# Attention and MoE on one core: moving low-part subtractions from GpSimd to VectorE

## The chip, the core and the metric

The kernel runs on one core of a Trainium2 chip. Its engines have a queue each and run side by side: TensorE (PE in the profile; PEld are its weight loads), VectorE (DVE), ScalarE (ACT), GpSimd (POOL), and SyncE (SP), which issues the DMAs. The metric is the device time of one execution in microseconds (us).

## The reference

A block-sparse attention and a feed-forward layer behind it, cut to what is computed:

```python
scores = 0.125 * q @ k.T              # per batch (4) and head (8), 768 x 768, head size 64
scores = where(mask, scores, -1e9)    # band, first and last blocks, 3 sampled blocks per row
attn = exp(scores - max) / (sum + 1e-9)
x = heads_side_by_side(attn @ v)      # 3072 x 512
h = x @ w_in                          # 512 -> 2048
g = where(h >= 1, h, where(h <= -1, 0, (h + 1) ** 2 / 4))
out = g @ w_out                       # 2048 -> 512
```

## The kernel before

All matmuls that matter run in a shortened fp32 format (F32R). A value is split into a high part, which is the value cast to that format, and a low part, which is the value minus the high part; products of two split values are the sum of three matmuls (or of two, where one side holds both parts in its rows).

**Attention.** 32 heads, one after the other. For each head, matmuls (L267) give all scores into the `pa` buffers, VectorE takes row maxima of them (L272, twelve per head), joins them (L276), TensorE turns them (L280), and VectorE writes them as rows of the operand QA (L283, once per head; the first head has two). Only then can the head's final scores (L303, L304) start; ScalarE takes exponentials (L308) into `pt`. For heads of pairs 0 to 4, the first ten (called whole), these go straight into the product with v in full precision (L333). For the other 22 heads, ScalarE casts the high part ph (a line of the helper `rounded`, L196), VectorE subtracts the low part pl (L316), GpSimd sums the exponentials into `acc` (L323, five per half head), and the products with v take two matmuls (L335, L336). v itself is split for these 22 heads: `split` in `head` lets ScalarE cast the high part into half of `vn` and subtracts the low part into the other half (L243). VectorE also adds the two halves of the product (L345), reduces `acc` (L358), and splits queries and keys (L228) and the results x (L387, L395).

**Weights.** w_in and w_out arrive as 64-bit floats and are converted in 32 pieces of 128x512 (`convert`): a load to `raw`, one step on ScalarE (L168), four on VectorE (L169, L170, L172, L174) in a buffer `cva` of which there are two, then `split`: ScalarE casts the high part into `wi` (w_in, 16 pieces, kept on the chip) or `w` (w_out, 16 pieces, written to DRAM behind it by L448), and the low part is subtracted (L180). The buffer `cva` is free when that subtraction is done; ScalarE's L168 of the piece after next waits for it.

**Feed-forward.** For each half of a batch, 16 steps: matmuls (L457 to L459) into `hp`, ScalarE and VectorE form g (L463, L466, L469), cast it (L196) and subtract its low part gl (L478), and L485 to L487 multiply with `w`. The first half of the first batch runs while w_out is still being converted.

**What sets the order.** `at` puts every step on a plan with a due time, and the steps are issued by due time. A scheduler then puts each engine's instructions into one fixed queue, by these priorities and its own picture of when operands and buffers are ready. On an engine, an instruction that waits holds up everything behind it. So a change of engine alone also changes the order.

Of the kernel before, what the change touches and what calls it, by code (L numbers as in the profile page):

```python
# [13 lines left out]
ALU = mybir.AluOpType  # L14
# [23 lines left out]
def body(ctx, tc, qk_t, v, sampled_blocks, moe_w_in, moe_w_out, ind, cm, negd, ident, fold, out):  # L38
    nc = tc.nc
# [11 lines left out]
    op = pool("op", 1)  # L51
# [21 lines left out]
    def f(ap):  # L73
        return ap.bitcast(F32)
# [82 lines left out]
    def convert(t, src, dst, done=None):  # L157
        st = {}

        def load():  # L160
            st["raw"] = cv.tile([128, 512, 2], I32, name="raw", bufs=3)
            Q_RAW.dma_start(out=st["raw"], in_=src.bitcast(I32).rearrange("p (c w) -> p c w", w=2))

        def bits():
            raw = st["raw"]
            lo32, hi32 = raw[:, :, 0], raw[:, :, 1]
            a = st["a"] = cv.tile([128, 512], I32, name="cva", bufs=2)
            nc.scalar.activation(out=f(a), in_=f(hi32), func=AF.Abs)  # L168
            nc.vector.tensor_scalar(out=f(a), in0=f(a), scalar1=CLO, scalar2=CHI, op0=ALU.max, op1=ALU.min)  # L169
            nc.vector.tensor_scalar(out=a, in0=a, scalar1=3, scalar2=0x3FFFFFFF,  # L170
                                    op0=ALU.logical_shift_left, op1=ALU.bitwise_and)
            nc.vector.scalar_tensor_tensor(out=a, in0=hi32, scalar=-0x40000000, in1=a,  # L172
                                           op0=ALU.bitwise_and, op1=ALU.bitwise_or)
            nc.vector.scalar_tensor_tensor(out=a, in0=lo32, scalar=29, in1=a,  # L174
                                           op0=ALU.logical_shift_right, op1=ALU.bitwise_or)

        def split():
            hi, lo = dst()
            rounded(CH, hi, f(st["a"]))
            nc.gpsimd.tensor_tensor(out=lo, in0=f(st["a"]), in1=f(hi), op=ALU.subtract)  # L180
            if done:
                done()

        conv.append((t, load, bits, split))
# [5 lines left out]
    def rounded(eng, dst, src):  # L190
        if eng is nc.vector:
            eng.tensor_copy(out=dst, in_=src)
        elif eng is nc.gpsimd:
            eng.tensor_scalar(out=dst, in0=src, scalar1=1.0, scalar2=0.0, op0=ALU.mult, op1=ALU.add)
        else:
            eng.copy(out=dst, in_=src)  # L196

    def head(i, n0, b, h, pst):
# [7 lines left out]
        st = {}  # L206
# [33 lines left out]
        def split(pl, n, src, hi, lo):  # L240
            t = st[n] = pl.tile([128, T, 128], F32R, name="vn")
            rounded(nc.scalar, t[:, :, hi], st[src])
            nc.gpsimd.tensor_tensor(out=t[:, :, lo], in0=st[src], in1=f(t[:, :, hi]), op=ALU.subtract)  # L243

        def v_whole():
            st["vn"] = VW[e]
# [5 lines left out]
        if whole:  # L252
            at(n0 - G["vw"], v_whole)
        else:
            at(n0 - G["vs"], split, vp, "vn", "lv", o0, o1)
# [372 lines left out]
```

## Time and profile before

| | us |
|---|---|
| median of 3 runs | 993.7 (993.34 to 997.28) |
| the profiled execution | 991.61 |
| its span, first to last instruction | 989.8 |
| TensorE busy | 947.2 (96%) |
| VectorE busy | 735.9 (74%) |
| ScalarE busy | 637.2 (64%) |
| GpSimd busy | 323.5 (33%) |

Busy time is the time in which an engine has an instruction under way; instructions that overlap count once. A group of instructions is given with its count, its busy time in sum, the mean of one in ns, and the idle time of its engine just before, with what ended it. Where a stretch of the span is named, it is in us from the first instruction.

### The profile page before, as it was taken

The page shows a single profiled execution, that of the slowest core. Times are in us where ns is not written, and L with a number is a line of the kernel's source. Part 1 is how long each engine was busy: PE and PEld are TensorE (multiplying, and loading weights), DVE is VectorE, ACT ScalarE, POOL GpSimd, SP SyncE. Part 2 cuts the span into 40 slices and gives each one's busy share as a digit, 9 for nine tenths or more (in the row PEclk, how much of TensorE's full clock was granted, in tenths as well). Part 3 has the DMA queues.
Part 4 walks back from the last instruction along what each step waited for, and adds up shares of the span by engine and source line. Part 5 has one row for each costly group of instructions (what it writes and reads, how often), then busy time and mean ns, then how long its engine had stood idle before and what let it go on. Part 6 is the DMA issues. An engine that isn't in the chain of part 4 may idle for free.

```text
span 989.8 us, 14583 instructions
## 1 busy us (share of the span) xinstructions
PE 947.2 (96%) x4687; PEld 830.4 (84%) x4687; DVE 735.9 (74%) x1349; ACT 637.2 (64%) x1302; POOL 323.5 (33%) x283
## 2 busy tenths in 40 slices
PE   5898899999899999999999999999999999999998
PEld 3666567778779989999989999998999899899996
DVE  5888887679998887888888897888888885422222
ACT  3676666666667666777767676866777676533433
POOL 1222120225554344444544444344544444000000
PEclk9999999999999999999999999999999999999999
DMA  6666676753455454656455454655546442434442
GB/s 196 200 182 184 190 207 204 228 180 103 155 170 172 128 141 129 186 151 174 136 143 175 133 150 137 184 158 152 156 130 187 116 124 86 154 128 128 160 128 96
DMA packets 56216, 154.43 MB, mean 156 GB/s; under 512 B 9612, under 2 KB 17952, under 8 KB 56140
## 3 DMA queue, kind: packets, MB, share of 16 engines
q1 hardware_dynamic: 56100, 153.48, 52.1%
q8 instruction: 37, 0.61, 0.3%
q14 instruction: 39, 0.32, 0.1%
q10 hardware_dynamic: 40, 0.03, 0.0%
HBM read 100.92 MB, written 14.81 MB: 117 GB/s over the span
## 4 chain that ended last, share of the span: by engine, by line
PE 70%; DVE 7%; ACT 2%; issue 1%; POOL 0%; POOLq 0%; ACTq 0%; DVEq 0%
PE oa L485 8%; PE oa L487 8%; PE oa L486 8%; PE hp L457 7%; PE hp L458 7%; PE hp L459 7%; PE po L335 5%; PE pa L303 4%; PE pa L304 4%; PE po L336 4%; PE pa L267 4%; DVE pl L316 2%; DVE mc L272 1%; PE pa L459 1%; PE pa L458 1%
## 5 line engine op out<-in xcount | busy, mean ns | idle before, releaser
L323 POOL TENSOR_TENSOR acc<-acc,pt 128x384 f32<-128x384 f32 x176 | 206.6, 1174 | 189.9 <-ACT pt L308 146.2
L272 DVE TENSOR_REDUCE mc<-pa 128x1 f32<-128x384 f32 x384 | 203.3, 549 | 20.4 <-PE pa L267 17.1
L196 ACT CAST ph<-pt 128x384 fp32r<-128x384 f32 x264 | 135.8, 514 | 94.4 <-PE po L335 90.1
L316 DVE TENSOR_TENSOR pl<-pt,ph 128x384 fp32r<-128x384 f32 x264 | 166.9, 632 | 33.3 <-ACT ph L196 32.4
L308 ACT ACTIVATE pt<-pa 128x384 f32<-128x384 f32 x288 | 140.5, 489 | 49.6 <-PE pa L304 41.6
L457 PE MATMUL hp<-x,wi 128*128 128x384 f32 x448 | 156.3, 349 | 5.4 <-DVE r L469 5.3
L485 PE MATMUL oa<-w,gh 128*128 128x512 f32 x384 | 153.3, 399 | 0.3 <-ACT gh L196 0.3
L459 PE MATMUL hp<-x,wi 128*128 128x384 f32 x448 | 152.1, 340 | 0.0
L458 PE MATMUL hp<-x,wi 128*128 128x384 f32 x448 | 152.0, 339 | 0.0
L487 PE MATMUL oa<-w,gl 128*128 128x512 f32 x384 | 151.5, 394 | 0.0
L486 PE MATMUL oa<-w,gh 128*128 128x512 f32 x384 | 150.8, 393 | 0.0
L267 PE MATMUL pa<-KA,QA 88*128 88x384 f32 x384 | 139.4, 382 | 8.8 <-DMA QA<-qkh 5.9
L469 DVE SCALAR_TENSOR_TENSOR r<-r,hp 128x384 f32<-128x384 f32 x112 | 61.8, 552 | 74.6 <-ACT r L466 74.4
L478 DVE TENSOR_TENSOR gl<-r,gh 128x384 fp32r<-128x384 f32 x128 | 91.0, 711 | 30.2 <-ACT gh L196 28.1
L267 PEld LDWEIGHTS pa<-KA,QA 88*128 88x128 f32 x384 | 73.4, 193 | 33.2 <-DVE mc L272 11.2
L303 PE MATMUL pa<-QA,KA 102*128 102x384 f32 x288 | 99.7, 346 | 0.7 <-DVE mc L272 0.4
L463 ACT ACTIVATE r<-hp,half_c 128x384 f32<-128x384 f32 x112 | 65.1, 581 | 52.3 <-PE hp L459 49.2
L304 PE MATMUL pa<-QB,KB 128*128 128x384 f32 x288 | 98.3, 341 | 0.0
L335 PE MATMUL po<-ph,vn 128*128 128x384 f32 x264 | 91.9, 348 | 4.7 <-DVE xun L345 3.9
L457 PEld LDWEIGHTS hp<-x,wi 128*128 128x128 f32 x448 | 85.0, 190 | 12.3 <-DVE r L469 7.8
L323 POOL TENSOR_TENSOR acc<-pt 128x384 f32<-128x384 f32 x44 | 45.6, 1037 | 136.7 <-ACT pt L308 132.9
L336 PE MATMUL po<-pl,vn 128*128 128x384 f32 x264 | 88.8, 336 | 0.0
(97 smaller groups left out, 1665.7 us busy)
## 6 DMA issues: line engine op xcount, KB each, us to landing
w<-wo_dram SPq DMA_DIRECT2D x112, 512.0 KB
qk<-in_qk_t_dram SPq DMA_DIRECT2D x32, 384.0 KB
raw<-in_moe_w_in_dram SPq DMA_DIRECT2D x16, 512.0 KB
raw<-in_moe_w_out_dram SPq DMA_DIRECT2D x16, 512.0 KB
wo_dram<-w SPq DMA_DIRECT2D x16, 512.0 KB
lv<-in_v_dram SPq DMA_DIRECT2D x32, 192.0 KB
KA<-qkh SPq DMA_DIRECT2D x32, 192.0 KB
QA<-qkh SPq DMA_DIRECT2D x32, 192.0 KB
```

The lines of the kernel that those rows point to most:

```text
L267: nc.tensor.matmul(out=pm[:, 0:HALF], lhsT=QAi[0:KM, t * 128:(t + 1) * 128], rhs=KAi[0:KM, kh * HALF:(kh + 1) * HALF], start=True, stop=True)
L272: nc.vector.reduce_max(out=st["mc"][:, t, kh:kh + 1], in_=st.pop(("pm", t, kh))[:, 0:HALF], axis=AX.X)
L308: nc.scalar.activation(out=p, in_=st.pop(("ps", c))[:, 0:HALF], func=AF.Exp, scale=SCALE)
L316: (nc.gpsimd if i < 2 * H and c in PL1 else nc.vector).tensor_tensor(out=pl, in0=st["p", c], in1=f(st["ph", c]), op=ALU.subtract)
L323: nc.gpsimd.tensor_tensor(out=st["acc", hf], in0=prev, in1=st["p", c], op=ALU.add)
L335: nc.tensor.matmul(out=po, lhsT=st["vn"][:, c], rhs=st["ph", c], start=(c == 0), stop=False)
L457: nc.tensor.matmul(out=hv, lhsT=wi[:, j, 0, fs], rhs=x[:, 0], start=(j == 0), stop=False)
L458: nc.tensor.matmul(out=hv, lhsT=wi[:, j, 0, fs], rhs=x[:, 1], start=False, stop=False)
L459: nc.tensor.matmul(out=hv, lhsT=wi[:, j, 1, fs], rhs=x[:, 0], start=False, stop=(j == NP - 1))
L485: nc.tensor.matmul(out=o, lhsT=gh[:, ts], rhs=w[:, 0], start=(fi == 0), stop=False)
L486: nc.tensor.matmul(out=o, lhsT=gh[:, ts], rhs=w[:, 1], start=False, stop=False)
L487: nc.tensor.matmul(out=o, lhsT=gl[:, ts], rhs=w[:, 0], start=False, stop=(fi == NF - 1))
```

## The change

The two subtractions of `split` go to VectorE's queue; what they read and write stays the same. GpSimd keeps the sums L323, and some setting of constants at the start.

```diff
@@ -177,7 +177,7 @@
         def split():
             hi, lo = dst()
             rounded(CH, hi, f(st["a"]))
-            nc.gpsimd.tensor_tensor(out=lo, in0=f(st["a"]), in1=f(hi), op=ALU.subtract)
+            nc.vector.tensor_tensor(out=lo, in0=f(st["a"]), in1=f(hi), op=ALU.subtract)
             if done:
                 done()
 
@@ -240,7 +240,7 @@
         def split(pl, n, src, hi, lo):
             t = st[n] = pl.tile([128, T, 128], F32R, name="vn")
             rounded(nc.scalar, t[:, :, hi], st[src])
-            nc.gpsimd.tensor_tensor(out=t[:, :, lo], in0=st[src], in1=f(t[:, :, hi]), op=ALU.subtract)
+            nc.vector.tensor_tensor(out=t[:, :, lo], in0=st[src], in1=f(t[:, :, hi]), op=ALU.subtract)
```

In the rows of the queues, the number behind QA is its buffer's, mc and mr are a head's maxima, rc holds reciprocals, xun a result before its division, and r the value from which g is formed.

First place: VectorE between a head's last maximum and its L283, the one at 121.45 us in the trace of before. Before:

```order
L272 TENSOR_REDUCE mc<-pa 128x1 x12
L372 RECIPROCAL rc<-rc 24x32
L276 TENSOR_TENSOR mr<-mc 128x6
L172 SCALAR_TENSOR_TENSOR cva<-raw,cva 128x512
L283 TENSOR_TENSOR QA_113<-pa,nd 6x768
```

The same place after:

```order
L272 TENSOR_REDUCE mc<-pa 128x1 x12
L180 TENSOR_TENSOR wi<-cva,wi 128x512
L276 TENSOR_TENSOR mr<-mc 128x6
L174 SCALAR_TENSOR_TENSOR cva<-raw,cva 128x512
L169 TENSOR_SCALAR cva<-cva 128x512
L283 TENSOR_TENSOR QA_113<-pa,nd 6x768
L372 RECIPROCAL rc<-rc 24x32
L180 TENSOR_TENSOR wi<-cva,wi 128x512
```

One subtraction now stands ahead of L276, two steps of a conversion instead of one ahead of L283, and a second subtraction behind it.

Second place: VectorE ahead of the L283 that stands at 278.8 us in the trace of before, while w_out is being converted. Before:

```order
L276 TENSOR_TENSOR mr<-mc 128x6
L369 TENSOR_SCALAR rc<-pa 24x32
L316 TENSOR_TENSOR pl<-pt,ph 128x384
L372 RECIPROCAL rc<-rc 24x32
L283 TENSOR_TENSOR QA_113<-pa,nd 6x768
L316 TENSOR_TENSOR pl<-pt,ph 128x384
L169 TENSOR_SCALAR cva<-cva 128x512
L228 TENSOR_TENSOR qk<-qk,qkh 128x768
```

After:

```order
L276 TENSOR_TENSOR mr<-mc 128x6
L369 TENSOR_SCALAR rc<-pa 24x32
L316 TENSOR_TENSOR pl<-pt,ph 128x384
L372 RECIPROCAL rc<-rc 24x32
L180 TENSOR_TENSOR w<-cva,w 128x512
L316 TENSOR_TENSOR pl<-pt,ph 128x384
L283 TENSOR_TENSOR QA_113<-pa,nd 6x768
L469 SCALAR_TENSOR_TENSOR r<-r,hp 128x384
```

A subtraction and one pl more stand ahead of L283, and r is formed earlier, ahead of the next conversion.

Third place: VectorE in a steady head, behind the end of a half head's product. Before:

```order
L316 TENSOR_TENSOR pl<-pt,ph 128x384
L345 TENSOR_TENSOR xun<-po,otmp 64x384
L478 TENSOR_TENSOR gl<-r,gh 128x384
L316 TENSOR_TENSOR pl<-pt,ph 128x384
L272 TENSOR_REDUCE mc<-pa 128x1 x2
```

After:

```order
L316 TENSOR_TENSOR pl<-pt,ph 128x384
L345 TENSOR_TENSOR xun<-po,otmp 64x384
L243 TENSOR_TENSOR vn<-lv,vn 128x6x64
L478 TENSOR_TENSOR gl<-r,gh 128x384
L316 TENSOR_TENSOR pl<-pt,ph 128x384
L272 TENSOR_REDUCE mc<-pa 128x1 x2
```

The subtraction for v stands alone between L345 and L478; the rest keeps its order. TensorE's order differs in the first quarter of its queue only.

## Rows read from the trace of the kernel before

**Rows 1.** The page's first part: busy time, share, instructions of each engine.
```profile
PE 947.2 (96%) x4687; PEld 830.4 (84%) x4687; DVE 735.9 (74%) x1349; ACT 637.2 (64%) x1302; POOL 323.5 (33%) x283
```

**Rows 2.** By stretch: length, busy PE, PEld, DVE, ACT, POOL; PEclk, DMA, GB/s.
```profile
15.50:153.60 138.10, 124.42 (x490) 88.83 (x490) 119.21 (x226) 92.81 (x187) 26.22 (x19) 0.99 0.68 197
153.60:208.40 54.80, 53.72 (x245) 42.72 (x244) 37.23 (x70) 33.70 (x66) 7.42 (x6) 1.00 0.63 196
208.40:243.40 35.00, 32.28 (x151) 27.92 (x150) 29.22 (x51) 24.04 (x49) 15.87 (x13) 0.95 0.48 149
243.40:278.80 35.40, 31.33 (x145) 25.64 (x144) 35.21 (x55) 21.81 (x46) 18.70 (x15) 0.95 0.48 155
278.80:309.30 30.50, 28.97 (x154) 26.59 (x153) 28.74 (x51) 22.05 (x47) 15.35 (x13) 1.00 0.52 166
309.30:850.00 540.70, 537.39 (x2827) 495.10 (x2826) 441.07 (x811) 382.65 (x797) 236.46 (x210) 1.00 0.50 146
```

**Rows 3.** The chain of waits in 243.4 to 278.8, by engine and line.
```profile
by line: DVE pl L316 18.9%; DVE mc L272 14.5%; issue 12.2%; DVE cva L172 10.3%; DVE cva L174 10.1%; DVE cva L169 6.9%; DVE r L469 5.4%; DVE gl L478 4.4%; DVE cva L170 4.1%; DVE QA L283 2.7%; PE hp L457 1.7%; PE po L335 1.6%; DVE psum L358 1
```

**Rows 4.** GpSimd's groups, whole span: busy us, mean ns, idle before, releaser.
```profile
L243 POOL TENSOR_TENSOR vn<-lv,vn 128x384 fp32r<-128x384 f32 x22 | 24.0, 1089 | 16.6 <-ACT vn L196 16.6
L180 POOL TENSOR_TENSOR wi<-cva,wi 128x512 fp32r<-128x512 f32 x16 | 22.3, 1401 | 96.2 <-ACT wi L196 96.2
```

**Rows 5.** Instructions of a line: duration in ns, least/median/greatest; first and last start.
```profile
L316 DVE TENSOR_TENSOR pl<-pt,ph x264: 482/552/1376, 214.5 to 842.9; 128x384 fp32r<-128x384 f32 x132
L169 DVE TENSOR_SCALAR cva<-cva x32: 399/421/1519, 20.5 to 280.3; 128x512 f32<-128x512 f32 x32
L172 DVE SCALAR_TENSOR_TENSOR cva<-raw,cva x32: 662/692/1651, 24.0 to 283.1; 128x512 int32<-128x512 int32 x32
L174 DVE SCALAR_TENSOR_TENSOR cva<-raw,cva x32: 616/688/1771, 24.9 to 284.2; 128x512 int32<-128x512 int32 x32
```

**Rows 6.** VectorE's groups in 15.5 to 153.6.
```profile
L172 DVE SCALAR_TENSOR_TENSOR cva<-raw,cva 128x512 int32<-128x512 int32 x20 | 15.6, 782 | 0.4
L174 DVE SCALAR_TENSOR_TENSOR cva<-raw,cva 128x512 int32<-128x512 int32 x20 | 15.6, 781 | 0.3
```

**Rows 7.** Instructions in time at 121 to 123: start, duration, idle before.
```profile
121.45 0.95 DVE L283 TENSOR_TENSOR QA<-pa,nd 6x768 fp32r<-6x768 f32 x1
...
122.45 0.45 PE L303 MATMUL oa<-QA,KA 102*128 102x384 f32 x1 [1.35 <-DVE QA L283]
```

**Rows 8.** Waits in 15.5 to 153.6: us in sum, times, longest.
```profile
DVE cva L169 <- ACT cva L168: 8.1, 4, 2.5
...
ACT cva L168 <- POOL wi L180: 6.0, 8, 1.4
```

**Rows 9.** The same in 153.6 to 208.4.
```profile
DVE cva L169 <- ACT cva L168: 10.1, 5, 3.1
```

**Rows 10.** Groups of VectorE, then of GpSimd, in 208.4 to 278.8.
```profile
L316 DVE TENSOR_TENSOR pl<-pt,ph 128x384 fp32r<-128x384 f32 x22 | 17.6, 800 | 1.6 <-ACT ph L196 1.6
...
L172 DVE SCALAR_TENSOR_TENSOR cva<-raw,cva 128x512 int32<-128x512 int32 x6 | 6.3, 1052 | 0.1
L478 DVE TENSOR_TENSOR gl<-r,gh 128x384 fp32r<-128x384 f32 x8 | 6.0, 748 | 1.7 <-ACT gh L196 1.7
L174 DVE SCALAR_TENSOR_TENSOR cva<-raw,cva 128x512 int32<-128x512 int32 x6 | 5.9, 979 | 0.1
...
L169 DVE TENSOR_SCALAR cva<-cva 128x512 f32<-128x512 f32 x6 | 4.0, 659 | 3.4 <-ACT cva L168 3.4
...
L180 POOL TENSOR_TENSOR w<-cva,w 128x512 fp32r<-128x512 f32 x7 | 10.7, 1533 | 11.5 <-ACT w L196 11.5
...
L243 POOL TENSOR_TENSOR vn<-lv,vn 128x384 fp32r<-128x384 f32 x2 | 2.8, 1388 | 0.0
```

**Rows 11.** VectorE's L478 in 309.3 to 850, then in 850 to 989.8.
```profile
L478 DVE TENSOR_TENSOR gl<-r,gh 128x384 fp32r<-128x384 f32 x78 | 60.6, 777 | 8.1 <-ACT gh L196 6.3
...
L478 DVE TENSOR_TENSOR gl<-r,gh 128x384 fp32r<-128x384 f32 x32 | 17.9, 559 | 18.5 <-ACT gh L196 18.4
```

## The prediction

> **What bounds the kernel now.** I read the page's engine shares first: TensorE 96%, VectorE 74%, GpSimd 33% [rows 1]. That is an average over stages with different limits, so the next view is the table of stretches, cut where a head's row of maxima is made (L283) [rows 2]. From 309.3 us to the end TensorE hardly waits: it is busy 537.39 of 540.7 us, while VectorE has 99.6 us idle. So time can only be won or lost ahead of 309.3 us, and there the stretches differ. Stretch one, 15.5 to 153.6: TensorE 124.42 of 138.1, VectorE 119.21; each waits for the other in turn. Stretch two, 153.6 to 208.4: TensorE 53.72 of 54.8, VectorE with 17.6 us idle. Stretch three, 208.4 to 278.8: in its second half VectorE is busy 35.21 of 35.4 us, and TensorE's weight loads fall to 25.64 of 35.4, against 495.10 of 540.7 later [rows 2]. The chain of waits there runs through VectorE: pl 18.9%, mc 14.5%, the conversions' L172, L174 and L169 10.3, 10.1 and 6.9% [rows 3]. So VectorE, which gets the new work, is the bound for some 35 us, half a bound for 170 us, and free otherwise.
>
> The Trainium skill (Trainium Kernel Development and Optimization, Performance Expectations) says that matmul busy time misleads, since matmuls are pipelined, and that the busy share of weight loads tells more. The trace agrees here: in 243.4 to 278.8 the matmuls leave 4.1 us open, the weight loads at the later rate (495.10 of 540.7 is 0.916; 25.64 / 0.916 = 28.0) leave 7.4; by the first a faster VectorE could give back at most 4.1 us there, by the second 7.4.
>
> **What moves, and its price.** 54 subtractions leave GpSimd: 32 of 128x512 (L180; the 16 for wi took 22.3 us) and 22 of 128x384 (L243, 24.0 us) [rows 4]. No row shows L180's form on VectorE. Bounds from the nearest: the 128x384 subtraction L316 has a median of 552 ns, the 128x512 two-input L174 688 ns and L172 692 ns [rows 5]. I take 0.69 for L180, which has L174's size, and 0.55 for L243, which has L316's. All 54 together are 32 x 0.69 + 22 x 0.55 = 34 us of VectorE's time. Three things stand against them: conversions come later in VectorE's queue, VectorE's own instructions are no longer stretched by these GpSimd subtractions, and much lies in idle time.
>
> **Stretch one.** In the new order 16 L180 stand ahead of the head that ends this stretch, but only 17 conversions instead of 20 (counted at L174). Added 16 x 0.69 = 11.0; three conversions less at 2 x 0.421 + 0.692 + 0.688 = 2.22 each (L170, of L169's form, taken at L169's median) [rows 5] take 6.7 away. Relief: L172 and L174 average 782 and 781 ns here, with L180 as GpSimd's main work; 20 x (0.090 + 0.093) = 3.7 [rows 6]. VectorE's load changes by +0.6. On the serial path of a head (last L272, L276, TensorE's turn, L283, first scores) the profile shows that such steps count: L283 takes 0.95 us and TensorE stands 1.35 us for it [rows 7]. With these durations the instructions between the last L272 and L283 grow by 2.8 us over the eight heads (1.5 of it in the last, where there were none; in the diff's first place 0.77), part of it under the turn. Against this, ScalarE waited 6.0 us here for GpSimd to give the cva buffer free, and VectorE 8.1 us for ScalarE's step behind that [rows 8]; a subtraction of 0.69 instead of about 1.29 frees it sooner, where VectorE comes to it at once. I take 0, between -6.0 (all of ScalarE's wait) and +4.3 (11.0 - 6.7, no relief).
>
> **Stretch two.** 8 L180, 1 L243 and three conversions more: 5.5 + 0.55 + 6.7 = 12.8 us. VectorE's 17.6 us of idle time are the cover. But 10.1 of these are waits for ScalarE's L168 [rows 9]; if they stay, 7.5 cover 12.8, and 5.3 show. Below, TensorE's 53.72 of 54.8 allows -1.1. I take 0, as TensorE is the nearer bound.
>
> **Stretch three.** 7 L180 and 2 L243: 4.8 + 1.1 = 5.9, and VectorE is full. Relief: over their medians, L316 stands 22 x 0.248 = 5.5 too long, L172 6 x 0.360 = 2.2, L174 6 x 0.291 = 1.7, L478 8 x 0.189 = 1.5, L169 6 x 0.238 = 1.4, together 12.3 us. Of GpSimd's 15.87 + 18.70 = 34.6 us [rows 2] the subtractions are 10.7 + 2.8 = 13.5, or 39%, and the sums stay; so 4.8 us go [rows 10]. The other 7.5, over these 48 instructions, are 0.16 each; the nine new ones meet the sums alike: 1.4. Net 5.9 - 4.8 + 1.4 = +2.5, and I put all of it on the path. Bounds: +7.3 (no relief), and -3.3 (the first half's 5.8 us of idle time [rows 2] hides that much of the new work, while all relief counts).
>
> **After that.** One L180 and one L243 up to 309.3: 1.2 us, VectorE idle 1.8: 0 to +1.2, taken as 0. The other 18 L243 (9.9 us) go into 99.6 us of idle time; in a steady head each stands between L345 and the gl and pl subtractions, which lose 0.55 but were stretched when GpSimd ran beside them: L478 averages 777 ns there and 559 when GpSimd is silent at the end [rows 11]. TensorE's order is the same there as before. 0. On GpSimd only sums are left, with more room; they are off the path.
>
> Sum: 0 + 0 + 2.5 + 0 = +2.5. The profiled execution took 991.6 us (span 989.8 and 1.8 around it), so 994.1 by its own time. The median of the runs is 993.7, 2.1 above that execution, so 996.2.
>
> **Rivals.** *Slower, VectorE stands still for ScalarE.* The added wait: each L180 needs ScalarE's cast, which is queued behind exponentials. GpSimd waited 96.2 us for it [rows 4] and it cost nothing, as nobody stood behind. Behind VectorE's L180 stand the reductions that free TensorE's score buffers, and L276 and L283. It decides from the point where VectorE reaches L180 before the cast's end. Price: VectorE's nearest wait for ScalarE's part of a conversion is 8.1 us over 20 in stretch one [rows 6, 8], 0.4 each: 16 x 0.4 = 6.4, and 9 x 0.2 = 1.8 in stretch three (0.2 as half of that, an estimate): 996.2 + 8.2 = 1004.4. For it: VectorE is near its limit there. Against: the scheduler put several instructions between cast and subtraction in most places.
>
> *Faster, relief beats load.* All of ScalarE's 6.0 us go, stretch two gives 1.1, stretch three 3.3: 993.7 - 10.4 = 983.3. For it: L172 and L174 stand at 1052 and 979 ns in stretch three [rows 10], and L168 waits for GpSimd. It decides where ScalarE's and VectorE's waits in [rows 8] lie on TensorE's path. Against: the sums stay, and VectorE's load does not fall.
>
> The Trainium skill (SBUF — State Buffer, Who interferes with whom) has a VectorE instruction with two SBUF inputs contend with a GpSimd instruction that reads SBUF, and the loser wait for the whole of the other; the trace agrees, by L478's 777 against 559. By that rule all lengthening in stretch one, where no sums run, goes with the subtractions, which is this rival's condition.
>
> *Slower in the steady heads:* L243 ahead of gl and pl is not hidden: 18 x 0.55 = 9.9, so 1006.1. Against it: VectorE's idle time, and the unchanged order of TensorE.
>
> That the change doesn't do what it says is out: in the built order GpSimd holds nothing but sums behind its start, and VectorE has the 32 and 22.
>
> **How the numbers follow.** A measurement of this kernel tells about 0.5% from no change, 5 us. My forecast of 996.2 is inside that: 0.45. Relief 0.17, and faster by over 0.5%. VectorE standing still 0.33 and the steady heads 0.05, both slower: 0.38. The bounds add up to 983.3 (-10.4) and 1011.8 (4.3 + 5.3 + 7.3 + 1.2 = +18.1); they do not all fall together, and the range of 986 to 1009 holds the rivals' middle and leaves out about 2 in 10.
>
> **What would show it.** Right: VectorE's busy time up by 10 to 20 us from 735.9; L172 and L174 near 0.69 in stretch one; L180 at 0.69 and L243 at 0.55 on VectorE; the head that ended at 153.6 within 4 us of it, the one at 278.8 some 2 to 4 us late; the same pace after 309.3. Wrong: waits of L180 for the casts (wi, w) over 5 us in sum; the head of 153.6 early by more than 4; or TensorE gaps behind 309.3 that grow with each head.

## The result, and the profile after

The changed kernel takes 984.22 us (median of 6 runs, 982.76 to 985.37); the kernel before, run beside it, 993.03 (6 runs, 989.69 to 997.28). The ratio is 0.991, 95% interval 0.9889 to 0.9931: faster by 0.9%, where 996.2 was forecast and 986 to 1009 given as the range. The time lies outside the range, on the other side of no change. The profiled execution took 983.67 us with a span of 981.8, 8.0 less than before.

The page's first part of the kernel after, beside [rows 1]:

```profile
PE 942.5 (96%) x4687; PEld 828.1 (84%) x4687; DVE 747.5 (76%) x1403; ACT 636.5 (65%) x1302; POOL 251.8 (26%) x229
```

and its VectorE groups for the moved work (busy us, mean ns of one, idle time just before, and what ended it), beside [rows 4]:

```profile
L243 DVE TENSOR_TENSOR vn<-lv,vn 128x384 fp32r<-128x384 f32 x22 | 14.1, 640 | 0.4 <-ACT vn L196 0.2
L180 DVE TENSOR_TENSOR w<-cva,w 128x512 fp32r<-128x512 f32 x16 | 10.8, 674 | 0.7 <-ACT w L196 0.7
L180 DVE TENSOR_TENSOR wi<-cva,wi 128x512 fp32r<-128x512 f32 x16 | 10.7, 677 | 4.5 <-ACT wi L196 4.5
```

VectorE is busy 11.6 us longer and the kernel is faster. The prices of the moved instructions are as forecast (0.68 us for L180; L243 has a median of 0.554 us, and a mean of 0.64). The next view is the table by stretch of the kernel after, cut where [rows 2] are cut:

```profile
15.50:153.60 138.10, 128.63 (x519) 94.67 (x519) 121.88 (x239) 94.95 (x192) 0.00 (x0) 0.99 0.65 190
153.60:208.40 54.80, 54.23 (x250) 44.12 (x249) 47.39 (x94) 36.39 (x71) 0.00 (x0) 1.00 0.73 234
...
309.30:850.00 540.70, 537.23 (x2826) 494.63 (x2825) 442.33 (x827) 380.49 (x795) 211.29 (x189) 1.00 0.49 146
```

In the first stretch TensorE gets through 519 matmuls instead of 490, in the second through 250 instead of 245, and behind 309.3 us through as many as before (2826 and 2827). So the gain is made early. The clearest measure of where is equal work: up to which time TensorE has done the first 500, 745, 951, 1050 and 1200 matmuls. Counted by line, these are the same matmuls in both kernels, but for one at 500 and one at 1050. The kernel before, then after (the count stands behind the busy time of PE, and a difference of one is a cut between two starts):

```profile
0.00:154.10 154.10, 128.97 (x500) 91.23 (x501) 127.20 (x247) 97.32 (x193) 29.72 (x28) 0.99 0.68 195
0.00:209.10 209.10, 182.89 (x745) 134.25 (x746) 164.62 (x317) 130.82 (x259) 37.14 (x34) 0.99 0.67 195
0.00:260.40 260.40, 228.11 (x951) 173.53 (x952) 210.11 (x389) 164.83 (x329) 61.09 (x54) 0.98 0.63 187
0.00:282.10 282.10, 249.10 (x1050) 190.24 (x1051) 231.65 (x426) 178.73 (x359) 73.69 (x63) 0.98 0.62 183
0.00:312.40 312.40, 277.88 (x1200) 216.54 (x1201) 260.19 (x475) 201.21 (x406) 89.13 (x75) 0.98 0.61 182
```

```profile
0.00:148.00 148.00, 127.00 (x501) 92.13 (x502) 123.92 (x249) 93.96 (x187) 3.51 (x9) 0.99 0.66 190
0.00:201.70 201.70, 180.13 (x745) 135.29 (x746) 171.86 (x343) 130.79 (x259) 3.51 (x9) 0.99 0.67 201
0.00:249.50 249.50, 223.08 (x951) 171.34 (x952) 215.45 (x415) 164.82 (x329) 19.23 (x22) 0.99 0.64 193
0.00:272.30 272.30, 243.85 (x1050) 188.29 (x1051) 236.88 (x455) 179.28 (x358) 26.15 (x29) 0.99 0.62 186
0.00:304.50 304.50, 273.11 (x1200) 214.34 (x1201) 268.06 (x511) 201.00 (x405) 38.99 (x39) 0.99 0.62 187
```

The differences are -6.1, -7.4, -10.9, -9.8 and -7.9 us. So stretch one gives 6.1, stretch two 1.3, stretch three first 3.5 more and then takes 3.0 back, and nothing happens behind it. TensorE's clock has a part in the 3.5 (see the account of stretch three), but does not make the gain: a second trace of the changed kernel, with the mean granted clock of the kernel before (0.995), has a span of 982.5 us, 7.3 less than 989.8.

What became of the waits of [rows 8] and [rows 9] is in the waits of 15.5 to 153.6 after (us in sum, times, longest):

```profile
DVE wi L180 <- ACT wi L196: 4.5, 4, 1.7
DVE cva L169 <- ACT cva L168: 3.3, 4, 1.9
ACT cva L168 <- DVE wi L180: 1.9, 2, 1.1
```

VectorE stood 8.1 us at L169 for ScalarE's L168, and now 3.3; ScalarE stood 6.0 us for GpSimd there, and now 1.9 for VectorE. In 153.6 to 208.4 VectorE's 10.1 us at L169 [rows 9] are gone altogether. The new wait, L180 for ScalarE's cast, is 4.5 us.

One place shows how that can reach TensorE. The kernel before at 125.5 to 130 (start, duration, engine, line, idle time before and releaser):

```profile
125.55 0.69 DVE L174 SCALAR_TENSOR_TENSOR cva<-raw,cva 128x512 int32<-128x512 int32 x1
125.65 1.73 POOL L180 TENSOR_TENSOR wi<-cva,wi 128x512 fp32r<-128x512 f32 x1 [7.78 <-ACT wi L196]
...
127.41 0.67 ACT L168 ACTIVATE cva<-raw 128x512 f32<-128x512 f32 x1 [1.35 <-POOL wi L180]
...
128.12 0.43 DVE L169 TENSOR_SCALAR cva<-cva 128x512 f32<-128x512 f32 x1 [1.88 <-ACT cva L168]
...
128.92 0.55 DVE L272 TENSOR_REDUCE mc<-pa 128x1 f32<-128x384 f32 x1
...
129.53 0.44 PE L267 MATMUL pa<-KA,QA 88*128 88x384 f32 x1 [0.82 <-DVE mc L272]
```

GpSimd's subtraction takes 1.73 us, during which ScalarE waits for `cva`, VectorE waits for ScalarE, and the first row maxima L272 of the next head stand behind VectorE's L169, although their matmuls (L267) ended in time. This head's L283 came 11.9 us behind its first L267; in the kernel after the same head takes 9.3. Over the eight heads of the stretch the sum of this time fell from 71.8 to 69.5 us, so this one head is all of it; the other half of the 4.4 us that stretch one gained by marks lies between an L283 and the next head's L267.

The 1.73 us are themselves the work of two engines. The least of GpSimd's L180 in this stretch takes 1.27 us; this one began 0.10 us after VectorE's L174, which took its usual 0.69. At 75 us it is the other way round: VectorE's L172 begins 0.16 us after GpSimd's subtraction, takes 1.65 us and ends 0.54 us after it.

```profile
75.14 1.27 POOL L180 TENSOR_TENSOR wi<-cva,wi 128x512 fp32r<-128x512 f32 x1 [1.69 <-ACT wi L196]
75.30 1.65 DVE L172 SCALAR_TENSOR_TENSOR cva<-raw,cva 128x512 int32<-128x512 int32 x1
```

So whichever began first kept its time here, and the other was held up by about as long as was left of it. The means of 782 and 781 ns [rows 6] are not 20 slow instructions each: two of each line took some 1.65 us, the other 18 about 0.69.

The second such place is in SyncE's queue. The kernel before at 87 to 95 (SPq is SyncE issuing DMAs):

```profile
87.41 0.33 SPq L162 DMA_DIRECT2D raw<-in_moe_w_in_dram  x1
87.83 0.47 SPq L221 DMA_DIRECT2D KA<-qkh  x1
88.34 0.59 SPq L221 DMA_DIRECT2D QA<-qkh  x1
...
94.77 0.76 PE L267 MATMUL pa<-KA,QA 88*128 88x384 f32 x3 [1.16 <-DMA QA<-qkh]
```

and the wait ahead of that load in 80 to 95:

```profile
SPq L162 <- DVE cva L174: 5.2, 1, 5.2
```

A late conversion frees `raw` late; the load of 512 KB that waits for it goes out right ahead of the moves of KA and QA, and TensorE has them 6.4 us after QA's issue; it stood 1.16 us for them. In the kernel after no load stands there, and it is 4.4 us:

```profile
88.39 0.59 SPq L221 DMA_DIRECT2D QA<-qkh  x1
...
92.83 0.68 PE L267 MATMUL pa<-KA,QA 88*128 88x384 f32 x3
```

### The profile page after: what moved, and what is told of

Read it like the earlier page. It is cut to its first block, busy times and chain, and to the rows that moved or that the text cites. A ratio compares the mean times of both kernels' runs of the same rounds, so it can differ in the third digit from the quotient of the medians.

```text
span 981.8 us, 14556 instructions
## 1 busy us (share of the span) xinstructions
PE 942.5 (96%) x4687; PEld 828.1 (84%) x4687; DVE 747.5 (76%) x1403; ACT 636.5 (65%) x1302; POOL 251.8 (26%) x229
## 4 chain that ended last, share of the span: by engine, by line
PE 85%; DVE 7%; ACT 3%; DMA 2%; issue 2%; SPq 0%; ACTq 0%; DVEq 0%
PE oa L485 8%; PE oa L487 8%; PE oa L486 8%; PE hp L457 8%; PE hp L459 7%; PE hp L458 7%; PE pa L267 7%; PE pa L303 5%; PE pa L304 5%; PE po L335 5%; PE po L336 4%; PE po L333 4%; DVE mc L272 2%; PE oa L333 2%; DMA QA<-qkh 1%
## 5 line engine op out<-in xcount | busy, mean ns | idle before, releaser
L323 POOL TENSOR_TENSOR acc<-acc,pt 128x384 f32<-128x384 f32 x176 | 201.7, 1146 | 233.0 <-ACT pt L308 195.1
L272 DVE TENSOR_REDUCE mc<-pa 128x1 f32<-128x384 f32 x384 | 202.5, 547 | 19.3 <-PE pa L267 16.1
L316 DVE TENSOR_TENSOR pl<-pt,ph 128x384 fp32r<-128x384 f32 x264 | 163.6, 620 | 34.7 <-ACT ph L196 34.0
L267 PE MATMUL pa<-KA,QA 88*128 88x384 f32 x384 | 138.3, 380 | 5.4 <-DMA QA<-qkh 3.8
L323 POOL TENSOR_TENSOR acc<-pt 128x384 f32<-128x384 f32 x44 | 46.5, 1058 | 345.5 <-ACT pt L308 345.5
L478 DVE TENSOR_TENSOR gl<-r,gh 128x384 fp32r<-128x384 f32 x128 | 84.3, 658 | 24.0 <-ACT gh L196 23.5
L267 PEld LDWEIGHTS pa<-KA,QA 88*128 88x128 f32 x384 | 73.1, 192 | 28.7 <-DVE mc L272 4.7
L335 PE MATMUL po<-ph,vn 128*128 128x384 f32 x264 | 91.4, 346 | 5.1 <-DVE xun L345 3.4
```

The source lines that it names most:

```text
L267: nc.tensor.matmul(out=pm[:, 0:HALF], lhsT=QAi[0:KM, t * 128:(t + 1) * 128], rhs=KAi[0:KM, kh * HALF:(kh + 1) * HALF], start=True, stop=True)
L272: nc.vector.reduce_max(out=st["mc"][:, t, kh:kh + 1], in_=st.pop(("pm", t, kh))[:, 0:HALF], axis=AX.X)
L316: (nc.gpsimd if i < 2 * H and c in PL1 else nc.vector).tensor_tensor(out=pl, in0=st["p", c], in1=f(st["ph", c]), op=ALU.subtract)
L323: nc.gpsimd.tensor_tensor(out=st["acc", hf], in0=prev, in1=st["p", c], op=ALU.add)
```

## The experiments

Three theories stood at first. A: the buffer `cva` comes free sooner. B: VectorE is relieved of GpSimd's subtractions beside it. C: the order alone, in which 17 conversions instead of 20 stand ahead of the tenth L283. Later came D: the loads of raw weights on SyncE's queue. V, in some of the later expectations, is the theory that the number of conversions which VectorE has in stretch one counts; and in the expectation of the second trace the letter C stands for something else, that the change takes away long waits that go with TensorE's half clock. All results in one table; stretch one is the time from the first to the tenth L283 in the profiled execution, the next column from the tenth to the sixteenth, and the fifth column VectorE's wait at L169 for ScalarE's L168 within stretch one. The last two columns are at equal work: the time between the starts of TensorE's 60th and 500th matmul, and of its 500th and 1200th. In brackets stands what TensorE lost in that time at its lower granted clock (1.2 instead of 2.4 GHz), which is half the time at that level. Each of these times is from one execution; the two traces of the changed kernel differ by 1.0, 1.9, 0.3 and 1.9 us in the four columns of times, so a difference of 1 us in stretch one by marks tells nothing.

| kernel | median us | ratio to before (95%) | conversions ahead of the tenth L283 | wait at L169 | stretch one | tenth to sixteenth | matmul 60 to 500 | matmul 500 to 1200 |
|---|---|---|---|---|---|---|---|---|
| before | 991.3 to 993.0 | 1 | 20 | 8.1 | 138.1 | 182.7 | 124.6 (1.7) | 158.4 (3.4) |
| after | 984.22 | 0.991 (0.9889 to 0.9931) | 17 | 3.3 | 133.7 | 179.1 | 118.1 (1.7) | 156.7 (0) |
| after, second trace | 980.81 | 0.9897 (0.9875 to 0.9919) | 17 | 3.1 | 132.7 | 181.0 | 117.8 (1.7) | 158.6 (3.4) |
| weights only | 981.66 | 0.9906 (0.9878 to 0.9933) | 17 | 3.1 | 132.5 | 179.2 | 117.4 (1.7) | 156.8 (1.7) |
| values only | 991.3 | 1.0002 (0.9983 to 1.0022) | 20 | 8.7 | 138.1 | 182.2 | 125.2 (3.4) | 158.0 (1.7) |
| each L180 twice | 986.09 | 0.9937 (0.9914 to 0.996) | 15 | 0 | 131.9 | 182.5 | 117.7 (1.7) | 159.4 (1.7) |
| before, three cva | 988.21 | 0.9967 (0.9946 to 0.9987) | 20 | 1.1 | 136.8 | 183.2 | 122.3 (3.4) | 160.3 (5.1) |
| GpSimd beside | 990.91 | 0.9992 (0.9974 to 1.001) | 17 | 0.6 | 135.1 | 185.3 | 120.6 (1.7) | 162.9 (5.1) |
| GpSimd beside, holding cva | 996.42 | 1.0047 (1.0031 to 1.0063) | 17 | 0.7 | 137.6 | 189.9 | 123.0 (1.7) | 167.5 (8.5) |
| held by a write | 981.33 | 0.9892 (0.9866 to 0.9918) | 16 | 2.8 | 133.3 | 182.4 | 118.1 (3.4) | 159.2 (3.4) |
| GpSimd takes 504 of 512 columns | 987.54 | 0.9953 (0.9937 to 0.9969) | 17 | 2.1 | 133.4 | 184.9 | 119.5 (1.7) | 161.6 (5.1) |
| before, raw loaded once | 973.35 | 0.9814 (0.9786 to 0.9843) | 17 | 0 | 120.3 | 182.5 | 106.9 (0) | 157.3 (5.1) |
| after, six more loads | 987.09 | 0.9955 (0.994 to 0.997) | 18 | 5.2 | 137.1 | 182.3 | 121.1 (1.7) | 160.2 (3.4) |
| weights only, three cva | 978.2 | 0.9866 (0.9845 to 0.9888) | 20 | 0 | 132.9 | 176.7 | 117.2 (1.7) | 154.3 (0) |

**Which half.** The kernel before with only L180 moved, and with only L243 moved.

```diff
-            nc.gpsimd.tensor_tensor(out=lo, in0=f(st["a"]), in1=f(hi), op=ALU.subtract)
+            nc.vector.tensor_tensor(out=lo, in0=f(st["a"]), in1=f(hi), op=ALU.subtract)
```

> Only L180 (weights, 32 subtractions) on VectorE, L243 (values) stays on GpSimd. Three theories share the gain of 8 to 9 us, which the profile shows ahead of 209 us: (A) the conversion buffer comes free sooner, so ScalarE and VectorE wait less; (B) VectorE is no longer lengthened by GpSimd's subtractions; (C) the order alone, with three conversions moved out of the first heads. All three say 984 to 987 here, since L180 is what runs ahead of 209 us and the order of the conversions is that of the changed kernel. If the values carry the gain, 990 to 994.

```diff
-            nc.gpsimd.tensor_tensor(out=t[:, :, lo], in0=st[src], in1=f(t[:, :, hi]), op=ALU.subtract)
+            nc.vector.tensor_tensor(out=t[:, :, lo], in0=st[src], in1=f(t[:, :, hi]), op=ALU.subtract)
```

> Only L243 (values, 22 subtractions) on VectorE, L180 stays on GpSimd. A, B and C: no gain, 991 to 994, the head marks at 153.6 and 208.4 us as before. A gain of over 4 us would speak against all three.

All of the gain is with the weights (0.9906), none with the values (1.0002). The median of the first, 981.66, lies below the 984 to 987 that all three theories gave, and so does the changed kernel's own second median, 980.81.

**What VectorE's load costs.** The changed kernel with each L180 done twice on VectorE: 32 more instructions. In its profile L180 has a mean of 680 ns for wi and 768 for w, so that they are some 23 us.

```diff
             nc.vector.tensor_tensor(out=lo, in0=f(st["a"]), in1=f(hi), op=ALU.subtract)
+            nc.vector.tensor_tensor(out=lo, in0=f(st["a"]), in1=f(hi), op=ALU.subtract)
```

> The changed kernel with each weight subtraction on VectorE done twice: 32 x 0.68 = 22 us more of VectorE's time, no contention, no GpSimd. It prices VectorE's load alone. VectorE has 16.2 us idle in 15.5 to 153.6, 7.4 in 153.6 to 208.4 and is nearly full up to 279: if idle time covers what it can, only the 7 in the last of these show, +5: 989. If it covers nothing, +22: 1006.

The ratio is 0.9937, against 0.991 and 0.9897 in the two comparisons of the changed kernel: 23 us of load cost 2.7 to 4.0 us, where 5 was the least forecast (986.09 against 989), and the intervals of the ratios overlap. Stretch one became no longer (117.7 against 118.1 at equal work), though VectorE's busy time in it rose from 117.62 to 121.82 us (its order has 14 L180 more and two conversions fewer there). Some 4 us more of VectorE's load did not lengthen stretch one.

**The buffer and the contention.** The kernel before with three `cva` buffers; and three forms of the changed kernel in which GpSimd does something in addition behind each cast or subtraction: a subtraction hi - hi into scratch (it reads beside VectorE), the same with `cva` as an operand (it also holds the buffer), and a memset of `cva` (it holds the buffer and only writes).

```diff
-            a = st["a"] = cv.tile([128, 512], I32, name="cva", bufs=2)
+            a = st["a"] = cv.tile([128, 512], I32, name="cva", bufs=3)
```

> The kernel before with three conversion buffers instead of two; the subtractions stay on GpSimd. A: ScalarE's waits of 15 us for GpSimd's release go, and 3 to 5 us of time with them, 986 to 988 where before is 991. If the release matters only where VectorE is loaded too, 990 to 992.

```diff
+            s = cv.tile([128, 512], F32, name="dmy", bufs=2)
+            nc.gpsimd.tensor_tensor(out=s, in0=f(hi), in1=f(hi), op=ALU.subtract)
```

> The changed kernel, and beside each L180 on VectorE one GpSimd subtraction of the same size (hi minus hi into a scratch tile), for which nobody waits; the order of all other engines is that of the changed kernel. Its result is not used. It brings back the contention of before and nothing else. B: a good part of the gain goes, 988 to 992, with L172 and L174 near 780 ns in the first heads. A and C: 984 to 986.

```diff
+            s = cv.tile([128, 512], F32, name="dmy", bufs=2)
+            nc.gpsimd.tensor_tensor(out=s, in0=f(st["a"]), in1=f(hi), op=ALU.subtract)
```

> As the run before it, but the GpSimd subtraction reads the conversion buffer (buffer minus hi), so the buffer comes free only when GpSimd is done, as in the kernel before; the order of all other engines is that of the changed kernel. Its result is not used. A: the gain goes, 990 to 995, with waits of ScalarE's L168 for GpSimd of about 15 us. B: the same as the run before it. C: 984 to 986 in both.

```diff
+            nc.gpsimd.memset(f(st["a"]), 0.0)
```

> The changed kernel, and behind each weight subtraction GpSimd writes zeros into the conversion buffer, reading nothing; the buffer comes free some 0.6 us later, when that is done. Late release without a second reader of SBUF. A: 985 to 988, a part of the 5.5 us that the held buffer cost. If only GpSimd's reads hurt: 984. The order of the other engines differs from the changed kernel in some places, so 2 us are not to be told from it.

The third buffer took VectorE's wait at L169 from 8.1 to 1.1 us, but gave a third of the gain in the median (988.21, where theory A had 986 to 988), and 2.3 of 6.5 us in stretch one at equal work (4.0 with TensorE's clock taken out). Its VectorE groups in stretch one show one thing that stands against it: in this order GpSimd's subtractions meet L174 more often, at 931 ns instead of 781 [rows 6], and 20 times 0.150 is 3.0 us.

```profile
L174 DVE SCALAR_TENSOR_TENSOR cva<-raw,cva 128x512 int32<-128x512 int32 x20 | 18.6, 931 | 0.2
L172 DVE SCALAR_TENSOR_TENSOR cva<-raw,cva 128x512 int32<-128x512 int32 x20 | 15.7, 786 | 0.5
```

GpSimd reading beside the changed kernel took the whole gain (0.9992), and holding the buffer in addition another 5.5 us (1.0047). But only 2.5 and 4.9 us of that are in stretch one at equal work, and much of the rest is TensorE's clock: between matmul 500 and 1200 it lost 5.1 and 8.5 us there and none in the changed kernel's first trace. Nor does the pair price the hold alone, since a GpSimd subtraction of two different operands is longer (the least takes 1.27 us, against 1.04 for hi - hi) and holds VectorE up longer; and where theory A had waits of some 15 us of ScalarE for GpSimd, they are 1.8 us in stretch one and 6.5 in the whole run. The first is not the contention of the kernel before, as was meant: the added subtraction starts with VectorE's own L180 and stretches that, while L172 and L174 stay at 689 and 733 ns. VectorE's L180 in 15 to 210 us, first with GpSimd reading beside it, then, in the kernel with the memset, with GpSimd writing:

```profile
L180 DVE TENSOR_TENSOR wi<-cva,wi 128x512 fp32r<-128x512 f32 x16 | 14.7, 921 | 4.3 <-ACT wi L196 4.3
```

```profile
L180 DVE TENSOR_TENSOR wi<-cva,wi 128x512 fp32r<-128x512 f32 x16 | 10.9, 683 | 1.3 <-ACT wi L196 1.2
```

And ScalarE's wait for that memset in its stretch one:

```profile
ACT cva L168 <- POOL cva L180: 10.2, 7, 2.0
```

With the memset ScalarE waited 10.2 us for GpSimd, more than in the kernel before, and lost nothing (0.9892, where theory A had 985 to 988 us and the median is 981.33): the wait as such had no price. VectorE stood at L169 for 2.8 us there, not 8.1. So theory A holds at most in part. That the hold costs where VectorE comes to L169 in that time and has the next head's L272 behind it is what the place at 125.5 us suggests; no run shows it by itself.

**Who subtracts, or the order.** VectorE subtracts 8 columns and GpSimd the other 504, so that the scheduler makes nearly the order of the changed kernel while GpSimd does the work of the kernel before.

```diff
+            nc.vector.tensor_tensor(out=lo[:, 0:8], in0=f(st["a"])[:, 0:8], in1=f(hi)[:, 0:8], op=ALU.subtract)
+            nc.gpsimd.tensor_tensor(out=lo[:, 8:512], in0=f(st["a"])[:, 8:512], in1=f(hi)[:, 8:512], op=ALU.subtract)
```

> The changed kernel, but VectorE subtracts only 8 of the 512 columns of each weight tile and GpSimd the other 504: contention, the late release of the conversion buffer and GpSimd's work are as before, VectorE's load is nearly as before, and the conversions stand three later, as in the changed kernel (17 ahead of the tenth row of maxima, 20 before). C (the order alone): 984 to 986. A and B (late release, contention): 990 to 994, no gain.

Stretch one is nearly as short as in the changed kernel (133.4 by marks, 119.5 against 118.1 at equal work), with GpSimd subtracting. The median of 987.54 lies between the 984 to 986 of theory C and the 990 to 994 of A and B. In this order ScalarE waits only 1.6 us for GpSimd, and L172 and L174 are not held up:

```profile
L172 DVE SCALAR_TENSOR_TENSOR cva<-raw,cva 128x512 int32<-128x512 int32 x17 | 11.6, 687 | 0.2
L174 DVE SCALAR_TENSOR_TENSOR cva<-raw,cva 128x512 int32<-128x512 int32 x17 | 11.4, 678 | 0.2
```

But VectorE is held up all the same, in its own eight columns:

```profile
L180 DVE TENSOR_TENSOR wi<-cva,wi 128x8 fp32r<-128x8 f32 x16 | 8.9, 555 | 6.7 <-ACT wi L196 6.5
```

Their median is 204 ns in the whole run and their greatest 1236. So contention alone (theory B) does not set stretch one; most of the gain there came with the order, and which conversions and maxima it moves is open. Behind the tenth L283 this kernel loses 2.2 us against the kernel before (184.9), of which 1.7 go with TensorE's clock, so no price of GpSimd's work can be read there.

**The raw loads.** The kernel before with the raw weights loaded once, and the changed kernel with six more loads of 512 KB, each directly ahead of a head's KA and QA moves.

```diff
-            st["raw"] = cv.tile([128, 512, 2], I32, name="raw", bufs=3)
-            Q_RAW.dma_start(out=st["raw"], ...)
+            if "raw" not in turns: ... Q_RAW.dma_start(out=st["raw"], ...)
```

> The kernel before with one edit: the 512 KB of raw weights are loaded once, and all 32 conversions read that one tile, so 31 loads are left out (and the output is that of wrong weights). The order has 17 conversions ahead of the tenth row of maxima (L283), as the changed kernel and the run with GpSimd subtracting 504 of 512 columns have; GpSimd subtracts. Theory D (what stretch one lost in the kernel before were the raw loads that stand ahead of the moves of QA, for which TensorE's L267 then waits): stretch one falls below that run's 133.4 us, to 130 to 132.5, and TensorE's waits for the DMA of QA are under 0.5 us there. Theory V (what counts is how many conversions VectorE has there): 133 to 134, as in that run. Stretch two in both: 54 to 55, as GpSimd still subtracts.

```diff
+            if 3 <= i <= 8:
+                Q_RAW.dma_start(out=dr.tile([128, 1024], I32, name=f"dm{i}"), in_=moe_w_in[0:128, 0:512].bitcast(I32))
             move(KAi[0:64], st["hi"][R])
```

> The changed kernel with six more loads of 512 KB (DRAM to DRAM, nobody reads them), one directly ahead of the KA and QA moves of each of the heads 3 to 8. The order then has 18 conversions ahead of the tenth row of maxima instead of 17. Theory D: each such load holds the moves up by some 1 to 2 us, as in the kernel before, and stretch one goes from 133.7 to 137 to 142 us, with TensorE's waits for the DMA of QA at 3 to 8 us; median 986 to 992 us. Theory V: one conversion more, at most 2.2 us: 133.7 to 135.9, no more DMA waits.

Their stretch one (length, busy time of PE, PEld, DVE, ACT, POOL, then PEclk, DMA share, GB/s):

```profile
15.11:135.40 120.29, 118.29 (x487) 88.22 (x487) 110.69 (x219) 89.75 (x183) 23.02 (x17) 1.00 0.50 136
```

```profile
13.93:151.01 137.08, 124.82 (x498) 90.98 (x498) 121.37 (x239) 92.23 (x186) 0.00 (x0) 0.99 0.75 222
```

Without the loads stretch one is 17.8 us shorter than in the kernel before, and 13.1 shorter than the 133.4 of the kernel in which GpSimd takes 504 columns, which has as many conversions ahead and GpSimd subtracting too; the second is the fairer comparison, since the order changed as well. TensorE stands only 2.0 us in it (120.29 less 118.29). That is far more than theory D had said (130 to 132.5), though ScalarE still waits 6.5 us for GpSimd there. Six more loads cost 3.4 us there (137.1 against 133.7) and 6.3 us in the median (987.09 against 980.81 in the same comparison). So the loads are on the path of stretch one. How they act was forecast wrongly: TensorE's waits for QA's DMA rose only from 1.2 to 2.0 us (3 to 8 were expected); more came through later row maxima (waits for L283 7.5 us instead of 5.2).

**A second trace, and a better kernel.** The changed kernel once more, and the kernel before with only L180 moved and three `cva` buffers.

```diff
-            a = st["a"] = cv.tile([128, 512], I32, name="cva", bufs=2)
+            a = st["a"] = cv.tile([128, 512], I32, name="cva", bufs=3)
...
-            nc.gpsimd.tensor_tensor(out=lo, in0=f(st["a"]), in1=f(hi), op=ALU.subtract)
+            nc.vector.tensor_tensor(out=lo, in0=f(st["a"]), in1=f(hi), op=ALU.subtract)
```

> The changed kernel once more, beside the candidate and for a second trace: 0.989 to 0.993. Theory C (the two half-speed stretches of TensorE's clock behind 208 us, 222 to 226 and 256 to 260 in the kernel before, go with long waits there, and the change takes these away): none of them between 208 and 280 us in this trace either, and matmul busy time within 1 us of 942.5. If the clock's fall was an accident of one profile: one or two here, and 945 to 947.

> The candidate: the kernel before with only L180 moved to VectorE, and a third cva buffer. The order has 20 conversions ahead of the tenth row of maxima, as the kernel before. If the buffer adds what it gave alone (0.9967) to the 0.9906 of the weights alone: 0.987, 979 us. If the early conversions take back what the later order gave (theories D and V alike): stretch one 136 to 138 us, and 0.993 to 0.996.

The second has 20 conversions ahead of the tenth L283, as the kernel before, and stretch one is 132.9 us all the same, where theories D and V gave 136 to 138. So C falls as it was put, and V with it: not the number of conversions ahead counts; nor do the loads, which come with the conversions, by themselves explain what the change gained. VectorE does not wait at L169 at all there, and L172 and L174 take 685 and 682 ns. Beside the kernel with three buffers and GpSimd subtracting it also says that the wait at L169 is not the whole of it. From the 60th to the 500th matmul, first with GpSimd subtracting, then with VectorE:

```profile
28.50:150.80 122.30, 112.02 (x441) 79.93 (x440) 108.91 (x205) 84.00 (x169) 24.52 (x18) 0.97 0.67 198
28.50:145.70 117.20, 108.05 (x442) 79.06 (x441) 110.78 (x221) 84.45 (x169) 0.00 (x0) 0.99 0.67 201
```

Both have 20 conversions ahead and at most 1.1 us of that wait, and moving L180 still gives 5.1 us there (3.4 with TensorE's clock taken out), against 7.2 with two buffers (124.6 to 117.4). All kernels in which GpSimd is silent or only writes, and which have the loads of the kernel before, take 117.2 to 118.1 us for these matmuls, whether that wait is 0 or 3.3 us.

Of the second trace's expectation one half came true: TensorE is busy 943.4 us, within 1 us of 942.5. The other did not: one fall of the clock stands between 208 and 280 us, in 213 to 219. So it is not shown that the change takes these falls away. With 978.2 us (977.03 to 979.28) against 980.81 (979.17 to 984.28) on the same chip it is the fastest kernel of this study that computes everything, by some 0.3% over the changed one; the intervals of the two ratios overlap.

## Why the prediction was wrong, step by step

**Stretch one: taken as 0, measured -6.1 by equal work (-4.4 at the mark of the tenth L283).** This step failed. It set ScalarE's 6.0 us [rows 8] against VectorE's load and the longer serial path, and let them cancel. Neither of the two came. VectorE's busy time in stretch one fell by 1.6 us (119.21 to 117.62), where +0.6 was worked out; the eight heads' time from L267 to L283 fell from 71.8 to 69.5 us, where the instructions ahead of L283 were to add up to 2.8; and more load has next to no price here (117.7 us against 118.1 with each L180 done twice). So what was to stand against the relief did not show. The lower bound of -6.0 was the right end as a number, but not by its own reason, which is luck: it priced ScalarE's wait, and with the memset 10.2 us of that wait cost nothing. What the runs show in its place is that taking the weights' subtractions off GpSimd is worth 7.2 us between the 60th and the 500th matmul with two buffers, and 5.1 (3.4 without the clock) where the wait at L169 had nearly gone already. Why is in part open: a third buffer alone gives 2.3 there (4.0 without the clock), and nearly the changed kernel's order, with GpSimd still subtracting, gives 5.1. How the gain divides between the hold, the instructions that were held up, the order, and loads that come at a better moment was not settled: each of them moves the others.

**Stretch two: taken as 0, bounds -1.1 to +5.3, measured -1.3 by equal work and -3.8 by marks** (54.8 to 51.0 between the tenth and the twelfth L283). The floor came from TensorE's busy time, 53.72 of 54.8. It nearly held as a statement on TensorE's work. It did not hold for the marks, since an L283 is an event on VectorE: 245 matmuls lie between the two marks before and 234 after. Such a mark is therefore a poor place to test a bound on TensorE.

**Stretch three: +2.5, measured -0.5 by equal work,** in two parts: -3.5 up to matmul 951 and +3.0 from there to 1200. The first part goes with TensorE's granted clock in this pair of traces. The kernel before at 222 to 228 and 255 to 261:

```profile
222.00:225.00 3.00, 2.97 (x10) 2.97 (x11) 0.99 (x1) 2.44 (x6) 2.36 (x3) 0.58 0.65 221
225.00:228.00 3.00, 3.00 (x15) 2.94 (x15) 2.34 (x5) 1.67 (x4) 2.44 (x2) 0.85 0.05 17
...
255.00:258.00 3.00, 1.52 (x4) 1.27 (x5) 2.97 (x8) 2.01 (x5) 0.87 (x1) 0.77 0.53 183
258.00:261.00 3.00, 3.00 (x13) 3.00 (x13) 3.00 (x3) 0.81 (x2) 3.00 (x3) 0.66 0.01 3
```

Here TensorE had stood for some 2 us and then worked at 1.2 GHz; 3 x (0.42 + 0.15 + 0.23 + 0.34) is 3.4 us of clock. The first trace after has no such row between 45 and 980 us. The second one has two, so that this part is not the change's: from 213 to 219 and from 282 to 288 us, for the same 3.4 us.

```profile
213.00:216.00 3.00, 2.84 (x13) 2.84 (x14) 1.81 (x3) 2.95 (x8) 1.50 (x2) 0.78 0.20 79
216.00:219.00 3.00, 3.00 (x13) 3.00 (x12) 2.82 (x5) 1.29 (x3) 0.53 (x1) 0.65 0.48 176
```

By equal work, the second trace has 745 and 1200 matmuls done at

```profile
0.00:200.60 200.60, 179.36 (x745) 135.20 (x746) 171.73 (x343) 130.77 (x259) 3.50 (x9) 0.99 0.67 202
0.00:305.20 305.20, 274.40 (x1200) 217.69 (x1201) 268.41 (x511) 200.95 (x405) 38.52 (x39) 0.98 0.61 186
```

or 104.6 us apart, against 103.3 before and 102.8 in the first trace after. With the clock's 3.4 us taken out of the first, the step is +2.9; in the second, with the same clock loss as before, +1.3. So the forecast of +2.5 for the load there agrees in sign, and about in size, if the clock's loss is all on the path, which no run shows. Its terms were not quite right: L172 and L174 stay at 901 and 1007 ns (before 1052 and 979), L316 falls from 800 to 702.

**After that: 0, and 0.** From the sixteenth L283 (336.3 and 328.4) to the end both kernels take 653.5 us. The relief of L478 is there, from 777 [rows 11] to 693 ns, and brings nothing, as TensorE is busy 537.23 of 540.7 us.

```profile
L478 DVE TENSOR_TENSOR gl<-r,gh 128x384 fp32r<-128x384 f32 x78 | 54.0, 693 | 1.4 <-ACT gh L196 1.0
```

**The rivals.** "VectorE stands still for ScalarE" had a chance of 0.33 and fell: L180 waited 4.5 and 0.7 us, just over the 5 us named as a sign, but these waits took the place of longer ones at L169 (8.1 and 10.1) and nothing came of them. The steady heads did not slow down. "Relief beats load" was right in its direction, in the numbers of its first two terms (-6.0 and -1.1 against -6.1 and -1.3) and in its time (983.3 against 984.2), and not in its third (-3.3). The close time is in part luck: the first term's reason was ScalarE's wait, and the clock of stretch three stood in for relief that was not there. The rule of the Trainium skill (SBUF — State Buffer, Who interferes with whom) named beside it agrees with these traces: L172 and L174 fall from 782 and 781 to 687 and 683 ns in stretch one, where GpSimd falls silent, L180 rises from 677 to 921 where GpSimd is made to read beside it, and the place at 75 us shows an instruction that ends only 0.54 us after GpSimd's. The rival was given 0.17, because the sums that stay on GpSimd were weighed for the whole kernel, though none run in stretch one (POOL 0.00 there now).

**What else was named.** Right: VectorE's busy time up by 10 to 20 us (11.6); L172 and L174 near 0.69 in stretch one; the durations of L180 and, by its median of 554 ns, L243; the same pace after 309.3. Seen as named for "wrong": the head of 153.6 early by more than 4 us (149.3), and L180's waits of 5.2 us in sum. The head of 278.8 was to be 2 to 4 us late, and stood at 272.6.

## What to carry to other kernels

Where an engine stands still for a second engine that stands for a third, the third one's work on that buffer can be on the path, even if the third is idle two thirds of the time: moving it to the busiest of the three can pay, and the busy times don't tell. Do not price a wait by its length: here 10.2 us of ScalarE's waiting cost nothing, and taking away 7.0 of VectorE's 8.1 us gave 2.3 us in stretch one (4.0 without the clock). Look at the single durations behind a mean: 0.1 us on each of 20 instructions was here two of 1.65 us. And compare two orders at equal work of the bounding engine, with its clock beside it, since marks on another engine slide.

## What the runs showed that was not expected

The weight loads on SyncE's queue are worth more than the change: with 31 of the 32 left out, stretch one is 120.3 us, against 138.1 before and 133.4 in the kernel nearest in order, though the DMA engines were busy only 0.68 of it before [rows 2]. A load ahead of a head's moves lengthened the time from QA's issue to its first matmul from 4.4 to 6.4 us in the place shown.

A GpSimd memset of 128x512 beside VectorE's two-input instructions left them as they were (L180 683 ns, L172 691), while a GpSimd subtraction of the same size brought L180 to 921. It was not without effect: the one-input L170, at most 429 ns in the changed kernel, reached 714 there.

TensorE's clock fell to half after the same wait of 1.7 us (L335 for L353) near 213 us in one trace of the changed kernel and not in the other.
